# Row sums in four column strips, and a reordered tail, in a decode block of attention plus bilinear GLU

## The chip, the cores and the metric

One core of one Trainium2 chip. The metric is device microseconds of the whole program, median of several runs, lower is better. All data is fp32.

## The reference, cut to what matters

```
x: [2, 1, 512]; 32 heads of 128; the last W = 2048 of 8192 cached positions are used
xn = layernorm(x)
q  = xn @ wq                                     # 512 x 4096
p  = softmax(q . k / sqrt(128)) per head         # k, v: 2 x 32 x 2048 x 128
A  = (p . v, heads side by side) @ wo            # 4096 x 512
Bf = ((xn @ w_gate) * (xn @ w_up)) @ w_down      # 512 x 1376, 1376 x 512
return x + A + Bf                                # 2 x 512
```

With two rows of x, nearly all of the work is reading k, v and the weights once: 159 MB.

## The kernel before

**The stream.** All weights and both caches lie in DRAM as one array, already in the order in which they are used. `loads()` is a table written by hand: each step n names a buffer and the fields that one DMA brings. A field is a k or v block of one head (4,096 columns of 128 partitions), a 512-column piece of `wq`, the 128 rows of `wo` that belong to one head (512 columns), or a 128-row piece of `w_down` (`wd`, 512 columns, 256 KB). Three buffers `step0` to `step2` of 13,824 columns take turns, and a smaller one, `extra`, is used twice. All these DMAs go through SP's one queue in the order of the table; `issue(upto)` puts them into the program, and each waits until the readers of the columns that it overwrites are done.

**Scores.** For each head VectorE multiplies the k block by the query (`products`, "step<-step,q") and sums over 128 elements (`sums`, "s<-step"). After four heads (a group g) `weights(g)` finds a maximum, with one matmul into PSUM tile `tr` ("tr<-both,ones"), and ScalarE takes the exponentials (p).

**Values.** `weigh(h)` is eight TensorE matmuls of 512 columns; they write four strips of 32 partitions of an `o_ps` bank in turn. When a group is complete, `fold` copies the bank to SBUF (ScalarE, "o_sb<-o_ps"), `gather` picks the rows with four matmuls ("gu<-cst,o_sb"), and `scaled` multiplies by the reciprocal sums ("oT<-gu,rec").

**Row sums.** The products with `wo` and `wd` are added up in PSUM in two ways. `add_rows` is one matmul of 512 columns, whose two output rows stand in partitions 0 and 1 of tile `acc`. `add_groups` is four matmuls of 128 columns, which write four 32-partition strips of `acc_g`, the first 128 columns of bank `q0`. Near the end VectorE adds `acc` and x into `acc_sb`, and `add_groups` with a 2x2 identity adds that to `acc_g`, which is what leaves the chip.

**Tail.** Step 21 brings V25, V26, V27 (and wo 26, 27, wd 3), step 22 V28 and V29 (and wo 28 to 31), step 23 V30 into `extra`, and step 24 V31 and then six wd pieces in three DMAs, into the columns of buffer 0 where K30 and K31 were. The code from line 557 on is the order of TensorE's work there. Each engine runs its instructions in the order of the code.

In the trace every instruction has line 197 (the recorder's), so groups are told apart by their tiles.

Of the kernel before, what the change touches and what calls it, by code (L numbers as in the profile page):

```python
# [4 lines left out]
AF = mybir.ActivationFunctionType  # L5
ALU = mybir.AluOpType
# [4 lines left out]
P = 128  # L11
B, D, H, DH, SK, F = 2, 512, 32, 128, 8192, 1376
W = min(4096, max(256, SK // 4))
HB = P // B
# [12 lines left out]
N = B * HG  # L27
M = 4 * N
CK, CO = J * DH, D
CX = B * NC + 4 * N + 4 * HG + 2 * NFB + 2  # L30
BUFS = 3
WIDTH = 13824
WIDTH_X = 4096
# [2 lines left out]
def loads():  # L36


    def units(kind, *ids):
        w = {"k": CK, "v": CK, "wo": CO, "wd": CO, "wq": HG * DH}[kind]  # L40
        return [(kind, i, w) for i in ids]

    def wq(g, *cs):
        return units("wq", *[(g, c) for c in cs])

    big = {
        1: units("k", 0, 1, 2),
        3: units("k", 3, 4) + units("v", 0),
        4: units("k", 5, 6) + units("v", 1),
        5: units("k", 7, 8) + units("v", 2),  # L50
    }
    k, v = 9, 3
    for n in range(6, 20):
        i = 1 + n % 2
        big[n] = units("k", *range(k, k + i)) + units("v", *range(v, v + 3 - i))
        k, v = k + i, v + 3 - i
    big[20] = units("k", 30, 31) + units("v", 24)
    big[21] = units("v", 25, 26, 27)
    big[22] = units("v", 28, 29)
    small = {  # L60
        1: wq(1, 0, 1, 2),
        3: wq(1, 3) + wq(2, 0, 1),
        4: wq(2, 2, 3) + units("wd", 0),
        5: wq(3, 0, 1, 2),
        6: units("wo", 0, 1, 2),
        7: wq(3, 3) + units("wo", 3) + wq(4, 0),
        8: units("wo", 4, 5, 6),
        9: units("wo", 7) + wq(4, 1, 2),
        10: wq(4, 3) + wq(5, 0, 1),
        11: units("wo", 8, 9, 10),  # L70
        12: units("wo", 11) + wq(5, 2, 3),
        13: wq(6, 0, 1, 2),
        14: units("wo", 12, 13, 14),
        15: units("wo", 15) + wq(6, 3) + wq(7, 0),
        16: units("wo", 16, 17, 18),
        17: units("wo", 19) + wq(7, 1, 2),
        18: wq(7, 3) + units("wd", 1, 2),
        19: units("wo", 20, 21, 22),
        20: units("wo", 23, 24, 25),
        21: units("wo", 26, 27) + units("wd", 3),  # L80
        22: units("wo", 28, 29, 30, 31),
    }
    out = [
        (0, "x", [("c", 0, CX)] + wq(0, 0, 1, 2, 3)),
        (1, 0, big[1] + small[1]),
        (2, 1, [(w, 0, NC * F) for w in ("wg", "wu")]),
        (3, 2, big[3] + small[3]),
    ]
    for n in range(4, 23):
        out += [(n, (1, 0, 2)[(n - 4) % 3], big[n] + small[n])]  # L90
    out += [
        (23, "x", units("v", 30)),
        (24, 0, units("v", 31)),
        (24, 0, units("wd", 4, 5)),
        (24, 0, units("wd", 6, 7)),
        (24, 0, units("wd", 8, 9)),
    ]
    return out
# [136 lines left out]
def build(nc, stream, x_nat, wd_rest, out):  # L235
# [2 lines left out]

    buf = [pr.sb(f"step{i}", [P, WIDTH]) for i in range(BUFS)]
    buf_x = pr.sb("extra", [P, WIDTH_X])  # L240
    xr = pr.sb("xr", [B, D])
    wr = pr.sb("wr", [FR, D])
    ones = pr.sb("ones", [P, P])
    mean_w = pr.sb("mean_w", [P, P])
    eps_t = pr.sb("eps", [P, 1])
    zero = pr.sb("zero", [P, 1])
    st = pr.sb("st", [P, 4, B])
    xc = pr.sb("xc", [P, B, NC])
    sq = pr.sb("sq", [P, B, NC])
    xn = pr.sb("xn", [P, NC, B])  # L250
    xnb = pr.sb("xnb", [P, NC, P])
    cst = pr.sb("cst", [P, CX])
# [9 lines left out]
    o_sb = [pr.sb(f"o_sb{i}", [P, FB]) for i in range(2)]  # L262
    h_sb = pr.sb("h_sb", [P, FB])
    hT = pr.sb("hT", [P, 4, NFB, B])
    acc_sb = pr.sb("acc_sb", [B, D])
    o_out = pr.sb("o_out", [P, P])

    o_ps = [pr.ps(f"o_ps{i}", [P, FB]) for i in range(2)]
    q_ps = [pr.ps(f"q{i}", [P, FB]) for i in range(2)]
    acc_t = pr.ps("acc", [P, FB])  # L270
    tr = pr.ps("tr", [P, FB])
    gu_ps = [pr.ps(f"gu{i}", [P, FB]) for i in range(2)]
    hT_ps, pk_ps = gu_ps
# [19 lines left out]

    issue(3)
    pr.load("ACT", wr, wd_rest)
    pr.load("ACT", xr, x_nat)

    dve.memset(mean_w, 1.0 / D)
    dve.memset(eps_t, EPS)
    dve.memset(zero, 0.0)  # L300
    dve.memset(ones, 1.0)
    dve.memset(mt, 0.0)
    dve.memset(both, 0.0)
    for t in gu_ps:
        dve.memset(t, 0.0)
    pool.memset(p_all, 0.0)

    c0 = got["c", 0]
    dve.tensor_copy(cst, c0)
    cut = [0]  # L310
    for w in (B * NC, 4 * N, 4 * HG, 2 * NFB, 2):
        cut.append(cut[-1] + w)
    xT = cst[:, cut[0] : cut[1]].rearrange("p (b c) -> p b c", b=B)
    pick = cst[:, cut[1] : cut[2]].rearrange("p (r n) -> p r n", r=4)
# [4 lines left out]
    id2 = cst[:B, cut[4] : cut[5]]  # L319

    dve.tensor_reduce(st[:, 0, :], xT, axis=AX.X, op=ALU.add)
    pe.matmul(tr[:, 0:B], mean_w, st[:, 0, :], start=True, stop=True)
    dve.tensor_tensor(
        xc, xT, tr[:, 0:B].unsqueeze(2).to_broadcast([P, B, NC]), op=ALU.subtract
    )
    dve.tensor_tensor(sq, xc, xc, op=ALU.mult)
    dve.tensor_reduce(st[:, 1, :], sq, axis=AX.X, op=ALU.add)
    pe.matmul(tr[:, 0:B], mean_w, st[:, 1, :], start=True, stop=True)
    act.activation(st[:, 2, :], tr[:, 0:B], AF.Sqrt, bias=eps_t)
    dve.reciprocal(st[:, 3, :], st[:, 2, :])  # L330
    dve.tensor_tensor(
        xn, xc.rearrange("p b c -> p c b"),
        st[:, 3, :].unsqueeze(1).to_broadcast([P, NC, B]), op=ALU.mult,
    )
    dve.tensor_copy(
# [72 lines left out]
    def fold(g):  # L408
        act.copy(o_sb[g % 2], o_ps[g % 2])
# [10 lines left out]
            oT[g % 2][:, lo:hi], pk_ps[:, lo:hi], rec[g % 2][:, lo:hi], op=ALU.mult  # L420
        )

    acc, acc_g = acc_t[:B, :], q_ps[(NG - 2) % 2][:, 0:P]
    n_acc, n_grp = 0, 0

    def add_rows(lhsT, rhs, last=False):
        nonlocal n_acc
        pe.matmul(acc, lhsT, rhs, start=(n_acc == 0), stop=last)
        n_acc += 1
# [33 lines left out]
    def turn():  # L463
        dve.tensor_copy(
            hT.rearrange("p i n b -> p (i n b)"), hT_ps[:, 0 : 4 * B * NFB]
        )
        add_rows(hT[:FR, NFC % 4, NFC // 4, :], wr)

    def down(c, add, **kw):
        add(hT[:, c % 4, c // 4, :], got["wd", c], **kw)  # L470

    def wo(h, add, **kw):
        g, hh = divmod(h, HG)
        add(oT[g % 2][:, B * hh : B * hh + B], got["wo", h], **kw)

    def score(h):
        products(h)
# [32 lines left out]
    for n in range(3, 21):  # L510
        ks, vs = has(n, "k"), has(n, "v")
        for h in late_wo:
            wo(h, add_rows)
        late_wo = []
        full = None
        for h in vs:
            if n > 3:
                weigh(h)
            if h % HG == HG - 1:
                full = h // HG  # L520
                fold(full)
        open_q += [(n, i) for i in has(n, "wq")]
        projections(ks[0] - 1)
        for c in has(n, "wd"):
            down(c, add_rows)
        if full is not None:
            gather(full)
        for x, h in enumerate(ks):
            products(h)
            if open_g is not None:  # L530
                denominators(open_g)
                open_g = None
            if n == 3 and x == 0:
                turn()
            projections(h)
            sums(h)
            if n == 20 and x == 1:
                weigh(25)
                weigh(26)
            if h % HG == HG - 1:  # L540
                weights(h // HG)
                open_g = h // HG
                if open_g:
                    reciprocals(open_g - 1)
            if x == 0 and full is not None:
                scaled(full)
                for i in range(full * HG, full * HG + HG):
                    if i in has(n, "wo") or i in has(n - 1, "wo"):
                        wo(i, add_rows)
# [13 lines left out]
    reciprocals(g)  # L563
    gather(g - 1)
    scaled(g - 1)
    down(3, add_rows)
    for h in GROUPS[g - 1]:
        wo(h, add_rows, last=(h == a - 1))
    issue(99)
    dve.tensor_tensor(acc_sb, acc, xr, op=ALU.add)  # L570
    weigh(a)
    add_groups(id2, acc_sb)
    weigh(b)
    weigh(c, last=True)
    fold(g)
    gather(g, 0, N - B)
    scaled(g, 0, N - B)
    for h in (a, b, c):
        wo(h, add_groups)
    weigh(d, bank=0, first=True)  # L580
    fold(0)
    for i in range(4, 6):
        down(i, add_groups)
    gather(0, N - B, N)
    scaled(g, N - B, N)
    for i in range(6, 8):
        down(i, add_groups)
    wo(d, add_groups)
    for i in range(8, NFC):
        down(i, add_groups, last=(i == NFC - 1))  # L590
    dve.tensor_copy(o_out, acc_g)
    pr.load("SP", out, o_out)
    pr.emit()
# [2 lines left out]
def laid_out(x):  # L596
# [16 lines left out]
        for b in range(B):  # L613
            xs[32 * n + b, o + n * B + b] = 1.0
    o += 2 * NFB
    for b in range(B):
        xs[b, o + b] = 1.0
# [58 lines left out]
```

## Time and profile before

| | |
|---|---|
| runs | 378.11, 378.38, 380.7 us; median 378.38 us |
| profiled execution | 378.41 us, span of the core 377.1 us |
| TensorE busy | 202.7 us (54%) |
| VectorE busy | 302.1 us (80%) |
| ScalarE busy | 15.1 us (4%) |
| SP's DMA queue | 159.35 MB, 98.2% of the span of 16 engines |
| mean granted TensorE clock | 0.718 |

Times in views of the trace are microseconds from the start of the span. 1.3 us of the program's time lie around the span (378.41 against 377.1). An fp32 matmul has two records in the trace, so "x16" of `o_ps` is one `weigh`. A row of the timeline has start, length, engine, operation, output and inputs with their shapes, and in brackets the idle time ahead of it and what ended it.

### The profile page before, as it was taken

The page shows a single profiled execution, that of the slowest core. Times are in us where ns is not written, and L with a number is a line of the kernel's source. Part 1 is how long each engine was busy: PE and PEld are TensorE (multiplying, and loading weights), DVE is VectorE, ACT ScalarE, POOL GpSimd, SP SyncE. Part 2 cuts the span into 40 slices and gives each one's busy share as a digit, 9 for nine tenths or more (in the row PEclk, how much of TensorE's full clock was granted, in tenths as well). Part 3 has the DMA queues.
Part 4 walks back from the last instruction along what each step waited for, and adds up shares of the span by engine and source line. Part 5 has one row for each costly group of instructions (what it writes and reads, how often), then busy time and mean ns, then how long its engine had stood idle before and what let it go on. Part 6 is the DMA issues. An engine that isn't in the chain of part 4 may idle for free.

```text
span 377.1 us, 2019 instructions
## 1 busy us (share of the span) xinstructions
PE 202.7 (54%) x880; PEld 59.3 (16%) x880; DVE 302.1 (80%) x165; ACT 15.1 (4%) x29; POOL 2.0 (1%) x5
## 2 busy tenths in 40 slices
PE   1651847623753557816457093381666374541996
PEld 1210122100220112101112020110111011010324
DVE  2059979999999987999599399969969995999400
ACT  1000100000000000000100000000000001000101
POOL 2000000000000000000000000000000000000000
PEclk9966756586685856858569756876568586675899
DMA  8999899998999999999999999999999999999994
GB/s 324 469 393 487 375 469 452 389 469 387 458 458 393 458 422 424 463 393 452 452 401 458 399 452 458 405 442 428 422 463 405 440 458 401 452 411 451 404 410 195
DMA packets 4300, 159.68 MB, mean 423 GB/s; under 512 B 482, under 2 KB 610, under 8 KB 1092
## 3 DMA queue, kind: packets, MB, share of 16 engines
q1 hardware_dynamic: 4176, 159.35, 98.2%
q10 hardware_dynamic: 116, 0.20, 0.2%
q8 instruction: 7, 0.11, 0.1%
q14 instruction: 1, 0.01, 0.0%
HBM read 159.49 MB, written 0.07 MB: 423 GB/s over the span
## 4 chain that ended last, share of the span: by engine, by line
DVE 44%; DMA 42%; PE 11%; issue 1%; another core or an unknown queue 1%; ACT 0%; SPq 0%; DVEq 0%
DMA step<-in_stream_dram 42%; DVE step L197 22%; DVE s L197 20%; PE acc L197 4%; PE o_ps L197 4%; PE q L197 2%; PE gu L197 1%; ACT o_sb L197 0%; PE tr L197 0%; DVE both L197 0%; DVE nm L197 0%; DVE h_sb L197 0%; DVE mt L197 0%; DVE mtt L197 0%
## 5 line engine op out<-in xcount | busy, mean ns | idle before, releaser
L197 DVE TENSOR_TENSOR step<-step,q 128x4096 f32<-128x4096 f32 x32 | 141.1, 4408 | 38.5 <-DMA step<-in_stream_dram 38.5
L197 DVE TENSOR_REDUCE s<-step 128x32 f32<-128x4096 f32 x32 | 141.4, 4418 | 0.8
L197 PE MATMUL o_ps<-step,p 128*32 128x512 f32 x496 | 89.4, 819 | 71.7 <-DMA step<-in_stream_dram 70.1
L197 PE MATMUL acc<-step,oT 128*2 128x512 f32 x56 | 39.7, 868 | 33.5 <-DVE oT L197 29.2
L197 PE MATMUL q<-step,xnb 128*128 128x512 f32 x56 | 40.6, 863 | 26.5 <-DVE step L197 18.9
L197 PEld LDWEIGHTS o_ps<-step,p 128*32 128x32 f32 x496 | 19.1, 139 | 123.3 <-DMA step<-in_stream_dram 76.9
L197 PEld LDWEIGHTS q<-step,xnb 128*128 128x128 f32 x56 | 13.4, 266 | 52.5 <-DVE step L197 24.1
L197 ACT ACTIVATE p<-s,zero 64x128 f32<-64x128 f32 x16 | 6.4, 399 | 266.9 <-DVE s L197 266.8
L197 PEld LDWEIGHTS acc<-step,oT 128*2 128x2 f32 x56 | 5.2, 105 | 62.0 <-DVE oT L197 30.1
L197 PE MATMUL gu<-step,xn 128*2 128x512 f32 (+1 forms) x48 | 9.7, 728 | 7.8 <-DMA step<-in_stream_dram 7.8
L197 PE MATMUL gu<-cst,o_sb 128*128 128x8 f32 (+2 forms) x72 | 9.5, 258 | 3.9 <-ACT o_sb L197 3.8
L197 PE MATMUL tr<-both,ones 128*128 128x24 f32 (+1 forms) x18 | 4.3, 317 | 12.7 <-DVE both L197 12.7
L197 DVE TENSOR_TENSOR oT<-gu,rec 128x8 f32<-128x8 f32 (+2 forms) x9 | 1.4, 159 | 12.1 <-PE gu L197 12.1
L197 PEld LDWEIGHTS gu<-cst,o_sb 128*128 128x128 f32 x72 | 8.7, 191 | 12.1 <-ACT o_sb L197 10.4
L197 DVE TENSOR_REDUCE nm<-tr 64x4 f32<-64x8 f32 x16 | 2.6, 163 | 6.6 <-PE tr L197 6.5
L197 ACT COPY o_sb<-o_ps 128x512 f32<-128x512 f32 x9 | 5.3, 585 | 49.8 <-PE o_ps L197 49.8
L197 PEld LDWEIGHTS tr<-both,ones 128*128 128x128 f32 x18 | 3.3, 229 | 23.3 <-DVE both L197 22.5
L197 PE MATMUL q<-extra,xnb 128*128 128x512 f32 x8 | 5.7, 878 | 1.2 <-DVE xnb L197 1.2
L197 PE MATMUL tr<-st,mean_w 128*128 128x2 f32 x4 | 1.2, 364 | 7.8 <-DVE st L197 7.8
L197 PEld LDWEIGHTS gu<-step,xn 128*2 128x2 f32 x48 | 2.2, 99 | 15.7 <-DMA step<-in_stream_dram 9.1
L197 PE MATMUL gu<-cst,h_sb 128*128 128x6 f32 x8 | 1.9, 362 | 4.4 <-DVE h_sb L197 4.4
L197 DVE TENSOR_TENSOR acc_sb<-acc,xr 2x512 f32<-2x512 f32 x1 | 0.7, 678 | 4.2 <-PE acc L197 4.2
(48 smaller groups left out, 43.8 us busy)
## 6 DMA issues: line engine op xcount, KB each, us to landing
step<-in_stream_dram SPq DMA_DIRECT2D x20, 6912.0 KB, 31.0
step<-in_stream_dram SPq DMA_DIRECT2D x1, 5504.0 KB, 34.4
step<-in_stream_dram SPq DMA_DIRECT2D x1, 5120.0 KB, 26.8
extra<-in_stream_dram SPq DMA_DIRECT2D x1, 2048.0 KB, 31.4
step<-in_stream_dram SPq DMA_DIRECT2D x1, 2048.0 KB, 28.0
step<-in_stream_dram SPq DMA_DIRECT2D x3, 512.0 KB, 21.4
extra<-in_stream_dram SPq DMA_DIRECT2D x1, 1056.0 KB, 6.0
wr<-in_wd_rest_dram ACTq DMA_DIRECT2D x1, 192.0 KB, 5.5
```

The source lines that it names most:

```text
L197: ins = getattr(e, method)(*args, **kw)
```

## The change

1. **Four strips.** `acc` is now a whole bank, zeroed at the start. `add_rows` takes a strip number j and writes partitions 32j and 32j+1; every wo row takes the strip of its head within the group (h % 4), except that heads 24, 25 and 26 take strip 0 and head 27 strip 1. `xr` (x, zero elsewhere), `acc_sb` and the identity (`id4`, two constant columns) stretch over 128 partitions.
2. **The final addition.** In the tail all wo rows but head 31's, and wd 1 to 7, go through `add_rows`. VectorE's addition of `acc` and x and `add_groups(id4, acc_sb)` come last, behind wd 8 and 9.
3. **wo rows of heads 26 and 27** go behind `fold(g)`, ahead of the gather that waits for that copy.
4. **Order of the stream.** wd 1 and 2 leave step 18, wd 3 leaves step 21; they come behind V31. The three last DMAs bring four, three and two pieces where each brought two.
5. **Four spare matmuls** (`keep_busy`) ahead of V25: 512 columns each, into a bank that nobody reads, with the scores of K30 as weights, so they wait for these.
6. **Layer norm** in one pass: sums of x minus a pivot and of its square go through one matmul instead of two in a row; two more constant columns hold the pivot.
7. **Memsets** of `zero`, `mt`, `both` and the new one of `xr` are on GpSimd, ahead of that of p; the load of x waits for the memset of `xr`.

```
         17: units("wo", 19) + wq(7, 1, 2),
-        18: wq(7, 3) + units("wd", 1, 2),
+        18: wq(7, 3),
...
-        21: units("wo", 26, 27) + units("wd", 3),
+        21: units("wo", 26, 27),
...
         (24, 0, units("v", 31)),
-        (24, 0, units("wd", 4, 5)),
-        (24, 0, units("wd", 6, 7)),
+        (24, 0, units("wd", 1, 2, 3, 4)),
+        (24, 0, units("wd", 5, 6, 7)),
         (24, 0, units("wd", 8, 9)),
...
+    spare = q_ps[(NG - 2) % 2]
+    n_acc, n_grp = [0] * 4, 0
+    def add_rows(lhsT, rhs, j, last=False):
+        pe.matmul(
+            acc[32 * j : 32 * j + B, :], lhsT, rhs, start=(n_acc[j] == 0), stop=last
+        )
+        n_acc[j] += 1
...
+    def keep_busy(behind, times):
+        for _ in range(times):
+            pe.matmul(
+                spare[:HB // 2, :], behind, xnb.rearrange("p c k -> p (c k)"),
+                start=True, stop=True,
+            )
...
             if n == 20 and x == 1:
+                keep_busy(s_t[1][:, 2, :], 4)
                 weigh(25)
                 weigh(26)
...
     scaled(g - 1)
-    down(3, add_rows)
-    for h in GROUPS[g - 1]:
-        wo(h, add_rows, last=(h == a - 1))
+    wo(a - 4, add_rows, 0)
+    wo(a - 3, add_rows, 0)
     issue(99)
-    dve.tensor_tensor(acc_sb, acc, xr, op=ALU.add)
     weigh(a)
-    add_groups(id2, acc_sb)
     weigh(b)
     weigh(c, last=True)
     fold(g)
+    wo(a - 2, add_rows, 0)
+    wo(a - 1, add_rows, 1)
     gather(g, 0, N - B)
     scaled(g, 0, N - B)
     for h in (a, b, c):
-        wo(h, add_groups)
+        wo(h, add_rows, h % HG)
     weigh(d, bank=0, first=True)
     fold(0)
-    for i in range(4, 6):
-        down(i, add_groups)
+    for i in range(1, 5):
+        down(i, add_rows, i % 4, last=(i == 4 - 1))
     gather(0, N - B, N)
     scaled(g, N - B, N)
-    for i in range(6, 8):
-        down(i, add_groups)
+    for i in range(5, 8):
+        down(i, add_rows, (i - 5), last=True)
+    dve.tensor_tensor(acc_sb, acc, xr, op=ALU.add)
     wo(d, add_groups)
     for i in range(8, NFC):
-        down(i, add_groups, last=(i == NFC - 1))
+        down(i, add_groups)
+    add_groups(id4, acc_sb, last=True)
     dve.tensor_copy(o_out, acc_g)
```

The order of the instructions shows this at three places. First TensorE from V24 (the first row below) to the wo rows of group 6; "-" is before, "+" is the change, and "hT" are the inputs of `wd`:

```order
-L197 MATMUL o_ps<-step,p 32x512 x24
+L197 MATMUL o_ps<-step,p 32x512 x8
+L197 MATMUL q<-xnb,s 32x512 x4
+L197 MATMUL o_ps<-step,p 32x512 x16
 L197 MATMUL tr<-both,ones 128x24
 L197 MATMUL o_ps<-step,p 32x512 x8
 L197 MATMUL tr<-both,ones 128x8
 L197 MATMUL gu<-cst,o_sb 128x8 x4
-L197 MATMUL acc<-step,hT 2x512
-L197 MATMUL acc<-step,oT 2x512 x4
+L197 MATMUL acc<-step,oT 2x512 x2
```

The four spare matmuls (q<-xnb,s) stand between V24 and V25, and three of the five serial `acc` matmuls have left the place ahead of V28.

Then the end of TensorE's program before, from V30 (`extra`) on:

```order
L197 MATMUL o_ps<-extra,p 32x512 x8
L197 MATMUL gu<-cst,o_sb 128x6 x4
L197 MATMUL q<-step,oT 2x128 x12
L197 MATMUL o_ps<-step,p 32x512 x8
L197 MATMUL q<-step,hT 2x128 x8
L197 MATMUL gu<-cst,o_sb 128x2 x4
L197 MATMUL q<-step,hT 2x128 x8
L197 MATMUL q<-step,oT 2x128 x4
L197 MATMUL q<-step,hT 2x128 x8
```

and in the change:

```order
L197 MATMUL o_ps<-extra,p 32x512 x8
L197 MATMUL acc<-step,oT 2x512 x2
L197 MATMUL gu<-cst,o_sb 128x6 x4
L197 MATMUL acc<-step,oT 2x512 x3
L197 MATMUL o_ps<-step,p 32x512 x8
L197 MATMUL acc<-step,hT 2x512 x4
L197 MATMUL gu<-cst,o_sb 128x2 x4
L197 MATMUL acc<-step,hT 2x512 x3
L197 MATMUL q<-step,oT 2x128 x4
L197 MATMUL q<-step,hT 2x128 x8
L197 MATMUL q<-acc_sb,cst 2x128 x4
```

Seven wd pieces stand as rows of `acc` around the last gather where four stood as groups, and the addition of `acc_sb` is the last thing that TensorE does.

Third, SP's last loads in the change, from step 18 (12,800 columns) to the store of the output:

```order
L197 DMA step<-in_stream_dram 128x12800
L197 DMA step<-in_stream_dram 128x13824 x2
L197 DMA step<-in_stream_dram 128x13312
L197 DMA step<-in_stream_dram 128x10240
L197 DMA extra<-in_stream_dram 128x4096
L197 DMA step<-in_stream_dram 128x4096
L197 DMA step<-in_stream_dram 128x2048
L197 DMA step<-in_stream_dram 128x1536
L197 DMA step<-in_stream_dram 128x1024
L197 DMA out_dram<-o_out 128x128
```

Steps 18 and 21 are 1,024 and 512 columns shorter, and the 1,536 columns stand again in the loads behind V31 (2,048, 1,536 and 1,024 where there were three of 1,024).

More of the change, by code (lines that the diff above doesn't have):

```diff
@@ L29 @@
 CK, CO = J * DH, D
-CX = B * NC + 4 * N + 4 * HG + 2 * NFB + 2
+CX = B * NC + 4 * N + 4 * HG + 2 * NFB + 2 + B
 BUFS = 3
@@ L240, in build @@
     buf_x = pr.sb("extra", [P, WIDTH_X])
-    xr = pr.sb("xr", [B, D])
+    xr = pr.sb("xr", [P, D])
     wr = pr.sb("wr", [FR, D])
@@ L247, in build @@
     st = pr.sb("st", [P, 4, B])
-    xc = pr.sb("xc", [P, B, NC])
-    sq = pr.sb("sq", [P, B, NC])
+    xc = pr.sb("xc", [P, 2, B, NC])
     xn = pr.sb("xn", [P, NC, B])
@@ L264, in build @@
     hT = pr.sb("hT", [P, 4, NFB, B])
-    acc_sb = pr.sb("acc_sb", [B, D])
+    acc_sb = pr.sb("acc_sb", [P, D])
     o_out = pr.sb("o_out", [P, P])
@@ L269, in build @@
     q_ps = [pr.ps(f"q{i}", [P, FB]) for i in range(2)]
-    acc_t = pr.ps("acc", [P, FB])
+    acc = pr.ps("acc", [P, FB])
     tr = pr.ps("tr", [P, FB])
@@ L295, in build @@
     pr.load("ACT", wr, wd_rest)
-    pr.load("ACT", xr, x_nat)
     dve.memset(mean_w, 1.0 / D)
     dve.memset(eps_t, EPS)
-    dve.memset(zero, 0.0)
     dve.memset(ones, 1.0)
-    dve.memset(mt, 0.0)
-    dve.memset(both, 0.0)
-    for t in gu_ps:
+    for t in gu_ps + [acc]:
         dve.memset(t, 0.0)
-    pool.memset(p_all, 0.0)
+    for t in (xr, zero, mt, both, p_all):
+        pool.memset(t, 0.0)
+    pr.load("ACT", xr[:B, :], x_nat)
     c0 = got["c", 0]
@@ L310, in build @@
     cut = [0]
-    for w in (B * NC, 4 * N, 4 * HG, 2 * NFB, 2):
+    for w in (B * NC, 4 * N, 4 * HG, 2 * NFB, 2, B):
         cut.append(cut[-1] + w)
@@ L318, in build, with per_row @@
     sel = cst[:, cut[3] : cut[4]]
[L319 to L324, printed above, removed]
-    )
[L326 to L329, printed above, removed]
+    id4 = cst[:, cut[4] : cut[5]]
+    pivot = cst[:, cut[5] : cut[6]]
+    def per_row(ap):
+        return ap.unsqueeze(2).to_broadcast([P, B, NC])
+    xd, sq = xc[:, 0], xc[:, 1]
+    dve.tensor_tensor(xd, xT, per_row(pivot), op=ALU.subtract)
+    dve.tensor_tensor(sq, xd, xd, op=ALU.mult)
+    dve.tensor_reduce(st[:, 0:2, :], xc, axis=AX.X, op=ALU.add)
+    pe.matmul(
+        tr[:, 0 : 2 * B], mean_w, st[:, 0:2, :].rearrange("p s b -> p (s b)"),
+        start=True, stop=True,
+    )
+    dve.tensor_tensor(xd, xd, per_row(tr[:, 0:B]), op=ALU.subtract)
+    dve.tensor_copy(st[:, 0:2, :].rearrange("p s b -> p (s b)"), tr[:, 0 : 2 * B])
+    dve.tensor_tensor(st[:, 2, :], st[:, 0, :], st[:, 0, :], op=ALU.mult)
+    dve.tensor_tensor(st[:, 1, :], st[:, 1, :], st[:, 2, :], op=ALU.subtract)
+    act.activation(st[:, 2, :], st[:, 1, :], AF.Sqrt, bias=eps_t)
     dve.reciprocal(st[:, 3, :], st[:, 2, :])
     dve.tensor_tensor(
-        xn, xc.rearrange("p b c -> p c b"),
+        xn, xd.rearrange("p b c -> p c b"),
         st[:, 3, :].unsqueeze(1).to_broadcast([P, NC, B]), op=ALU.mult,
@@ L421, in scaled @@
         )
[L423 to L429, printed above, removed]
+    spare = q_ps[(NG - 2) % 2]
+    acc_g = spare[:, 0:P]
+    n_acc, n_grp = [0] * 4, 0
[4 more added lines that the diff above has]
+        n_acc[j] += 1
     def add_groups(lhsT, rhs, last=False):
@@ L466, in turn, with down, wo @@
         )
[L467 to L472, printed above, removed]
+        add_rows(hT[:FR, NFC % 4, NFC // 4, :], wr, 0)
+    def down(c, add, *args, **kw):
+        add(hT[:, c % 4, c // 4, :], got["wd", c], *args, **kw)
+    def wo(h, add, *args, **kw):
         g, hh = divmod(h, HG)
-        add(oT[g % 2][:, B * hh : B * hh + B], got["wo", h], **kw)
+        add(oT[g % 2][:, B * hh : B * hh + B], got["wo", h], *args, **kw)
+    def keep_busy(behind, times):
+        for _ in range(times):
+            pe.matmul(
+                spare[:HB // 2, :], behind, xnb.rearrange("p c k -> p (c k)"),
+                start=True, stop=True,
+            )
     def score(h):
@@ L512, in build @@
         for h in late_wo:
-            wo(h, add_rows)
+            wo(h, add_rows, h % HG)
         late_wo = []
@@ L524, in build @@
         for c in has(n, "wd"):
-            down(c, add_rows)
+            down(c, add_rows, 1)
         if full is not None:
@@ L548, in build @@
                     if i in has(n, "wo") or i in has(n - 1, "wo"):
-                        wo(i, add_rows)
+                        wo(i, add_rows, i % HG)
                     else:
@@ L578, in build @@
     for h in (a, b, c):
-        wo(h, add_groups)
+        wo(h, add_rows, h % HG)
     weigh(d, bank=0, first=True)
     fold(0)
-    for i in range(4, 6):
-        down(i, add_groups)
+    for i in range(1, 5):
+        down(i, add_rows, i % 4, last=(i == 4 - 1))
     gather(0, N - B, N)
     scaled(g, N - B, N)
-    for i in range(6, 8):
-        down(i, add_groups)
+    for i in range(5, 8):
+        down(i, add_rows, (i - 5), last=True)
+    dve.tensor_tensor(acc_sb, acc, xr, op=ALU.add)
     wo(d, add_groups)
     for i in range(8, NFC):
-        down(i, add_groups, last=(i == NFC - 1))
+        down(i, add_groups)
+    add_groups(id4, acc_sb, last=True)
     dve.tensor_copy(o_out, acc_g)
@@ L615, in laid_out @@
     o += 2 * NFB
-    for b in range(B):
-        xs[b, o + b] = 1.0
+    for j in range(4):
+        for b in range(B):
+            xs[32 * j + b, o + b] = 1.0
+    xs[:, o + 2 :] = a[:, 0]
     cache = {
```

## The prediction

> **What bounds the kernel now.** I read the queue section of the page first, then the page's summary of the chain that ended last.
>
> ```profile
> q1 hardware_dynamic: 4176, 159.35, 98.2%
> DVE 44%; DMA 42%; PE 11%; issue 1%; another core or an unknown queue 1%; ACT 0%; SPq 0%; DVEq 0%
> ```
>
> SP's queue is at work for 98.2% of the span. The second row seems to say that VectorE is the bound, but a chain follows one release after another; where the queue never empties, the share of DVE in it costs nothing. So I read the chain in order of time (start, length, what).
>
> ```profile
> 308.73 38.89 DMA step<-in_stream_dram
> ...
> 347.66 5.86 PE o_ps L197 x32
> ...
> 357.47 3.96 PE acc L197 x9
> ...
> 363.90 3.62 PE o_ps L197 x32
> ...
> 370.32 1.76 PE o_ps L197 x16
> ...
> 373.80 1.25 PE q L197 x40
> ...
> 375.07 0.29 DVE o_out L197
> ```
>
> Step 21 (V25 to V27) lands at 308.73 + 38.89 = 347.62. Two loads earlier, step 19 released VectorE (the timeline's row):
>
> ```profile
> 314.95 4.42 DVE L197 TENSOR_TENSOR step<-step,q 128x4096 f32<-128x4096 f32 x1 [3.78 <-DMA step<-in_stream_dram]
> ```
>
> So two loads of 13,824 columns came in 347.62 - 314.95 = 32.7 us: 16.34 us each, or 0.605 us for 512 columns. From 347.62 on the chain is all TensorE. But it is hardly ahead of the transfers there, as the issues and their times to landing show (timeline rows, then rows of the DMA view of single stretches: KB, us to landing).
>
> ```profile
> 332.91 0.33 SPq L197 DMA_DIRECT2D step<-in_stream_dram  x1
> 333.28 0.43 SPq L197 DMA_DIRECT2D extra<-in_stream_dram  x1
> 341.69 10.06 SPq L197 DMA_DIRECT2D step<-in_stream_dram  x4
> ```
>
> ```profile
> step<-in_stream_dram SPq DMA_DIRECT2D x1, 5120.0 KB, 26.8
> extra<-in_stream_dram SPq DMA_DIRECT2D x1, 2048.0 KB, 31.4
> step<-in_stream_dram SPq DMA_DIRECT2D x1, 2048.0 KB, 28.0
> step<-in_stream_dram SPq DMA_DIRECT2D x1, 512.0 KB, 22.1
> ```
>
> ```profile
> L197 SPq DMA_DIRECT2D step<-in_stream_dram x26: 327/328/647, 1.2 to 351.3; - x26
> ```
>
> V28 lands at 332.91 + 26.8 = 359.7, V30 at 333.28 + 31.4 = 364.7, V31 at 341.69 + 28.0 = 369.7. The last row gives the start of the last load, 351.3, so wd 8 and 9 land at 351.3 + 22.1 = 373.4. The chain turns to V31 at 370.32, 0.6 us behind its landing, and ends its matmuls at 375.05, 1.6 us behind the last landing. So in the tail two lines run side by side, TensorE's and the queue's, and TensorE's is the later one by about half a microsecond. Whatever shortens TensorE by more than that meets the queue.
>
> **The change: the queue.** The stream carries the same fields, and 1 KB more of constants (8 bytes for each of 128 rows). Its end stays at 373.4. What moves is the order: three pieces ahead of V25 go behind V31. Everything from step 18 to V31 lands earlier by 0.605 us a piece: 1.21 us for steps 18 to 20, 1.82 us from step 21 on. V25 then lands at 345.8, V28 at 357.9, V30 at 362.9, V31 at 367.9. Behind V31 the pieces fill what is left up to 373.4, at 5.5 / 9 = 0.61 us each: wd 1 to 4 at 370.4, wd 5 to 7 at 372.2, wd 8 and 9 at 373.4. SP issues V31 when K30's scores are done and the wd loads when K31's are; both are over 20 us ahead of their landings, so no wait of SP reaches the queue.
>
> **The change: the spare matmuls and V25 to V27.** VectorE and TensorE meet at the maximum of the last group.
>
> ```profile
> 346.02 4.42 DVE L197 TENSOR_REDUCE s<-step 128x32 f32<-128x4096 f32 x1
> 351.26 0.23 DVE L197 TENSOR_SCALAR both<-cst,mc 128x16 f32<-128x16 f32 x1
> 353.45 0.40 PE L197 MATMUL tr<-both,ones 128*128 128x24 f32 x2
> 324.15 4.78 PE L197 MATMUL acc<-step,oT 128*2 128x512 f32 x6 [3.98 <-DVE oT L197]
> ```
>
> The wait for step 19 (the row at 314.95) now ends 1.2 us earlier; behind that it works without a pause, so K31's sums end at 349.2 instead of 350.44 and `both` is ready at 350.3 instead of 351.49. In the run before, TensorE came to that matmul only at 353.45, because V25 and V26 took 5.86 us (first chain row), against 3.62 us for two heads later on.
>
> ```profile
> 348.80:352.20 3.40, 3.40 (x20) 0.79 (x16) 2.56 (x5) 0.00 (x0) 0.00 (x0) 0.50 0.98 422
> 352.20:355.60 3.40, 3.40 (x30) 0.84 (x22) 0.99 (x5) 0.80 (x2) 0.00 (x0) 1.00 0.89 386
> 205.42:208.84 3.42, 1.54 (x4) 0.38 (x2) 3.38 (x2) 0.00 (x0) 0.00 (x0) 1.00 0.93 404
> 208.84:212.25 3.41, 0.00 (x0) 0.00 (x0) 2.12 (x1) 0.00 (x0) 0.00 (x0) 1.00 0.94 405
> 212.25:215.66 3.41, 0.00 (x0) 0.00 (x0) 0.00 (x0) 0.00 (x0) 0.00 (x0) 0.50 1.13 486
> ```
>
> These stretches show why (the granted clock is the third number from the end; the first behind the length is TensorE's busy time): 0.50 until a stretch of 3.4 us was busy throughout, then 1.00; and 1.00 kept through a stretch that was 45% busy, lost after one that was idle. Four spare matmuls are eight records; the six `acc` records in 4.78 us were about 0.86 us each at the low clock, so the spare ones take at most 6.9 us from 340.4 (K30's scores), to 347.3, and include at least one whole stretch: V25 and V26 then run at the high clock, 3.6 us. They end between 349.4 and 350.9, and the matmul for the maximum starts between 350.3 and 350.9 instead of 353.45. From there to the end of the gather took 357.47 - 353.45 = 4.0 us, so 354.9 at the latest; two wo rows in one strip are four records of 0.44 us (nine took 3.96), with 0.3 us for `scaled` 2.1 us. TensorE stands at V28 by 357.0, and V28 lands at 357.9. **It waits from here on**, so the gain of the spare matmuls and of the three rows taken out (2.6 us) buys nothing beyond these 0.9 us of slack.
>
> **The change: V28 to V31.** Durations come from these rows.
>
> ```profile
> 363.83 1.92 PE L197 MATMUL o_ps<-step,p 128*32 128x512 f32 x16
> 36.11 9.73 PE L197 MATMUL gu<-step,xn 128*2 128x512 f32 x48 [7.80 <-DMA step<-in_stream_dram]
> 372.11 0.58 ACT L197 COPY o_sb<-o_ps 128x512 f32<-128x512 f32 x1 [3.99 <-PE o_ps L197]
> 372.75 1.05 PE L197 MATMUL gu<-cst,o_sb 128*128 128x2 f32 x8 [0.27 <-ACT o_sb L197]
> 371.86 0.62 PE L197 MATMUL q<-step,hT 128*2 128x128 f32 x16
> 361.89 0.68 DVE L197 TENSOR_TENSOR acc_sb<-acc,xr 2x512 f32<-2x512 f32 x1 [4.22 <-PE acc L197]
> ```
>
> One head of `weigh` is 1.92 us for eight matmuls in four strips. The second row has the form of the new row sums: two output rows, 512 columns, three strips. One after another its 48 records would take 48 x 0.44 = 21 us; they took 9.73 us, half of it at the low clock. So strips overlap with two rows too, and I take 0.9 us for up to four wo or wd rows in different strips (two records of 0.43 us); the other end, no overlap, is a rival. V28 and V29 from 357.9 end at 361.5; V30 from 362.9 at 364.8. wo 26 and 27 take 0.9 us while the copy takes 0.6, so the gather starts at 365.7, and with `scaled` and three wo rows TensorE is done at 367.9, when V31 lands.
>
> From V31 at 367.9: `weigh` to 369.8, copy to 370.45. TensorE waits for wd 1 to 4 until 370.4, adds them by 371.3; gather to 372.35; wd 5 to 7 (landed 372.2) to 373.25; VectorE's addition, now over 128 partitions but still 512 elements each, 0.7 us, to 374.0. Meanwhile wo 31 and wd 8 and 9 (0.3 and 0.62 us) end at 374.15, and the addition through `id4` (four matmuls of that form, half of 0.62, and the way to VectorE: 0.35) at 374.5. **The copy to `o_out` starts at 374.5 instead of 375.07: 0.57 us earlier.** A second way gives the same: last landing 373.4, two pieces 0.62, `id4` 0.35, some 0.1 between.
>
> The Trainium skill, page "TensorE: Matmul & The Clock Gate", section "Measured speedup vs the span model", speaks against part of this: three column tiles gave 2.38 times there, not three. By it wd 5 to 7 would take 1.1 us, about 0.2 us more, and the program 378.0 us; of `acc` in three strips no run here shows the duration.
>
> **The change: edits at nothing.** Layer norm, memsets and the later load of x lie ahead of the first k block:
>
> ```profile
> 23.14 4.42 DVE L197 TENSOR_TENSOR step<-step,q 128x4096 f32<-128x4096 f32 x1 [12.99 <-DMA step<-in_stream_dram]
> ```
>
> VectorE had been idle for 12.99 us when K0 came, and of these the first projection of q (eight records of 0.86 us at most) takes 6.9: about 6 us are left before K0 would feel it. One matmul less stands against three small VectorE operations more, and x is not read before the last addition. wo rows in mid-stream use less of TensorE, which is not late there.
>
> **The sum.** 378.41 - 0.57 = 377.84 us against the profiled execution, which is 0.03 us from the median of 378.38: **377.8 us**, 0.15% below before, inside what a measurement of this kernel can tell from no change, about 1%. Bounds within this case: a clock that falls for one stretch in the new waits +0.5 (the wo rows and one gather at half speed, the rest of it in slack), and 0.4 either way for landings that I know to 0.1 us each. Its own range is 377.2 to 378.7.
>
> **The rivals.**
>
> *The clock goes cold in the new waits (slower).* TensorE now waits about 0.9 us for V28 and 1.4 us for V30, and where a stretch of 3.4 us falls below the 45% that held the clock, V31 starts at 0.50. Then `weigh` is 3.5 us, wd 1 to 4 1.7, the gather up to 2.1; with a whole busy stretch behind it the clock is back 3.4 to 6.8 us after V31. That puts the copy 1.7 to 2.8 us behind my 374.5: 379.5 to 380.6 us. Against it: I find no stretch of 3.4 us from 357.9 on with less than 1.9 us of work (56%). The Trainium skill, same page, section "What's actually happening", asks for an idle window of 3.4 us; the rows above agree, and no wait here is that long. It decides from a stretch under half busy before 368. Chance 0.06.
>
> *The stream slows.* Every load now starts 1 KB later in DRAM, and the first has rows of 8,456 bytes. From a slowdown of 0.16% (0.6 us of 372) the gain is gone; 1% gives 381.5. For it: nothing but that no load here started off the old grid. Against it: 5,120 KB took 359.7 - 347.62 = 12.1 us, at the rate of the 6,912 KB loads, though its rows are shorter; the rate doesn't hang on the form. Chance 0.09.
>
> *Strips with two rows don't overlap, so the change does not do what it says.* wo 26 and 27 then take 1.7 us, three rows 2.6, four 3.4: 0.9 + 1.7 + 2.6 + 1.7 less 1 us of cover puts the end 5 to 6 us behind mine, 383.5 us. The `gu` row speaks against it. Chance 0.04.
>
> *TensorE alone decided (faster).* If transfers are early enough everywhere, its own savings count: 353.45 - 350.4 = 3.0, three rows 2.6, the first `acc_sb` addition 0.3, less 0.9 for the longer end: 5 us, 373.4 us. Against it stands the last landing, 373.4, which allows no copy before 374.4. It needs a faster stream. Chance 0.07.
>
> **How the numbers follow.** Forecast 0.74, rivals 0.06, 0.09, 0.04, 0.07. Faster by over 1% (below 374.6) is the last rival, 0.07. Slower by over 1% (above 382.2) is the third and most of the second, which can be any size: 0.04 + 0.07 = 0.11. Within 1% is the rest, 0.82. The range reaches from 376.6 (half a microsecond of faster stream or a cheaper end) to 380.6, the upper end of the cold tail; slower streams and the two outer rivals are left out.
>
> **What would show each step.** Right: V25 lands near 345.8, V31 near 367.9, the last load still at 373.4; V25 and V26 in under 4 us at clock 1.00; TensorE idle ahead of V28 and V30 "<-DMA"; four wd rows in about 0.9 us; `o_out` at 374.5. The chain should show DMA, not TensorE, up to V31. Wrong: landings 16.4 us or more apart in mid-stream, a clock of 0.50 anywhere behind 358, or `acc` records that follow each other at 0.43 us in different strips.

## The result

The change runs in 377.89 us, median of 20 runs (377.68 to 378.08), against 378.47 us before (377.91 to 381.31, 20 runs): ratio 0.9967, 95% interval 0.9951 to 0.9983. The ratio is of means, and 6 of the 20 runs before lie between 380.7 and 381.3 us, where none of the change's does; the medians differ by 0.15%. Profiled execution: 377.87 us, span 376.5 us (before 378.41 and 377.1). The page of the change, queue section and summary of the chain:

```profile
q1 hardware_dynamic: 4176, 159.35, 98.3%
DVE 54%; DMA 40%; PE 4%; issue 1%; another core or an unknown queue 1%; SPq 0%; DVEq 0%
```

TensorE's share of the chain has fallen from 11% to 4%. The chain in order of time, its end:

```profile
349.41 20.93 DMA step<-in_stream_dram
370.34 0.04 issue
370.38 1.04 PE acc L197 x8
371.42 0.98 PE gu L197 x8
...
373.43 0.70 DVE acc_sb L197
...
374.17 0.45 PE q L197 x8
...
374.64 0.29 DVE o_out L197
```

Where before it was TensorE's from 347.62 on, it now is a transfer's until 370.34: the landing of wd 1 to 4. The copy to `o_out` starts at 374.64 instead of 375.07. The issues of V28, V30 and V31 on SP and the times to landing (rows of single stretches; the last is that of wd 8 and 9):

```profile
331.84 0.33 SPq L197 DMA_DIRECT2D step<-in_stream_dram  x1
332.22 0.42 SPq L197 DMA_DIRECT2D extra<-in_stream_dram  x1
340.63 10.06 SPq L197 DMA_DIRECT2D step<-in_stream_dram  x4
```

```profile
step<-in_stream_dram SPq DMA_DIRECT2D x1, 5120.0 KB, 26.2
extra<-in_stream_dram SPq DMA_DIRECT2D x1, 2048.0 KB, 30.7
step<-in_stream_dram SPq DMA_DIRECT2D x1, 2048.0 KB, 27.2
step<-in_stream_dram SPq DMA_DIRECT2D x1, 512.0 KB, 23.2
```

So V28 lands at 358.0 (before 359.7), V30 at 362.9 (364.7), V31 at 367.8 (369.7), and the last load, issued at 350.3, at 373.5 (373.4). TensorE in the timeline:

```profile
340.65 5.86 PE L197 MATMUL q<-xnb,s 128*32 128x512 f32 x8 [5.34 <-DVE s L197]
346.00 3.95 PE L197 MATMUL o_ps<-step,p 128*32 128x512 f32 x32
350.49 0.40 PE L197 MATMUL tr<-both,ones 128*128 128x24 f32 x2 [0.54 <-DVE both L197]
354.77 1.88 PE L197 MATMUL acc<-step,oT 128*2 128x512 f32 x4 [0.26 <-DVE oT L197]
358.11 3.64 PE L197 MATMUL o_ps<-step,p 128*32 128x512 f32 x32 [1.47 <-DMA step<-in_stream_dram]
363.01 1.92 PE L197 MATMUL o_ps<-extra,p 128*32 128x512 f32 x16 [1.26 <-DMA extra<-in_stream_dram]
364.75 1.03 PE L197 MATMUL acc<-step,oT 128*2 128x512 f32 x4
367.02 1.03 PE L197 MATMUL acc<-step,oT 128*2 128x512 f32 x6 [0.26 <-DVE oT L197]
367.89 1.92 PE L197 MATMUL o_ps<-step,p 128*32 128x512 f32 x16
```

The rows are the spare matmuls, V25 and V26, the maximum, wo 24 and 25, V28 and V29, V30, wo 26 and 27 in the pause (the time of `fold`'s copy, in which TensorE would wait for the gather's input), wo 28 to 30, V31. TensorE is idle for 1.47 and 1.26 us ahead of V28 and V30, "<-DMA" both times. The three wo rows (six records, 367.02) take 0.87 us until V31 starts; one after another they would take 2.6.

### The profile page after: what moved, and what is told of

The parts are those of the page before. It is cut to its first block, busy times and chain, and to the rows that moved or that the text cites. A ratio compares the mean times of both kernels' runs of the same rounds, so it can differ in the third digit from the quotient of the medians.

```text
span 376.5 us, 1954 instructions
## 1 busy us (share of the span) xinstructions
PE 194.0 (52%) x844; PEld 57.2 (15%) x844; DVE 302.9 (80%) x166; ACT 15.1 (4%) x29; POOL 2.6 (1%) x9
## 3 DMA queue, kind: packets, MB, share of 16 engines
q1 hardware_dynamic: 4176, 159.35, 98.3%
## 4 chain that ended last, share of the span: by engine, by line
DVE 54%; DMA 40%; PE 4%; issue 1%; another core or an unknown queue 1%; SPq 0%; DVEq 0%
DMA step<-in_stream_dram 40%; DVE step L197 27%; DVE s L197 25%; PE acc L197 2%; PE q L197 1%; DVE both L197 1%; PE tr L197 1%; DVE nm L197 0%; PE gu L197 0%; DVE mt L197 0%; DVE acc_sb L197 0%; DVE h_sb L197 0%; DVE mtt L197 0%; DVE rec L197 0%
## 5 line engine op out<-in xcount | busy, mean ns | idle before, releaser
L197 PE MATMUL o_ps<-step,p 128*32 128x512 f32 x496 | 95.4, 866 | 57.0 <-DMA step<-in_stream_dram 55.4
L197 PE MATMUL acc<-step,oT 128*2 128x512 f32 x62 | 23.7, 893 | 43.9 <-DVE oT L197 27.8
L197 PEld LDWEIGHTS o_ps<-step,p 128*32 128x32 f32 x496 | 21.1, 147 | 113.1 <-DMA step<-in_stream_dram 62.2
L197 PEld LDWEIGHTS acc<-step,oT 128*2 128x2 f32 x62 | 1.6, 82 | 54.0 <-DVE oT L197 28.5
L197 PE MATMUL q<-xnb,s 128*32 128x512 f32 x8 | 5.9, 903 | 5.3 <-DVE s L197 5.3
```

The source lines that it names most:

```text
L197: ins = getattr(e, method)(*args, **kw)
```

## Experiments

**Is it the order of the stream?** Theory: the landings of V31 and of the last load set the end. Rival: the gain is TensorE's shorter program (strips, pause, spare matmuls).

*The spare matmuls taken out.*

```
             if n == 20 and x == 1:
-                keep_busy(s_t[1][:, 2, :], 4)
```

> The change without its four spare matmuls; all else as in the change. Theory (the queue sets the end: V31 lands at 367.9 and the last load at 373.4 whatever TensorE does before): V25 and V26 run at the low clock at first, the matmul for the maximum starts at about 352 instead of 350.5, V28 starts within 0.5 us of its landing at 358, and the copy to o_out stays at 374.6; 377.9 us. Rival (the warm clock is what brings the gain): everything behind V25 is later by the 1.5 to 2 us, the copy at 375 or later, 378.4 us or more.

Measured: 377.85 us (377.77 to 378.00, 12 runs). V25, the maximum and V28 in its timeline:

```profile
345.94 5.79 PE L197 MATMUL o_ps<-step,p 128*32 128x512 f32 x32 [11.51 <-DMA step<-in_stream_dram]
351.66 0.40 PE L197 MATMUL tr<-both,ones 128*128 128x24 f32 x2
358.06 3.64 PE L197 MATMUL o_ps<-step,p 128*32 128x512 f32 x32 [0.24 <-DMA step<-in_stream_dram]
```

V25 and V26 take 5.79 us instead of 3.95, the maximum is 1.2 us later, and V28 starts when it lands, as in the change: the wait of 1.47 us has become one of 0.24. The spare matmuls buy nothing here.

*The old order of the stream in the changed program.*

```
-        18: wq(7, 3),
+        18: wq(7, 3) + units("wd", 1, 2),
-        21: units("wo", 26, 27),
+        21: units("wo", 26, 27) + units("wd", 3),
-        (24, 0, units("wd", 1, 2, 3, 4)),
-        (24, 0, units("wd", 5, 6, 7)),
+        (24, 0, units("wd", 4, 5)),
+        (24, 0, units("wd", 6, 7)),
...
+    down(3, add_rows, 3, last=True)          # behind scaled(g - 1)
...      # in words: wd 4, 5 as rows in the pause of fold(0), wd 6, 7 as rows behind the last gather
```

> The change with the stream order of before: wd 1 and 2 in step 18, wd 3 in step 21, and wd 4 to 9 in three loads of two pieces behind V31; strips, spare matmuls and the late addition as in the change. Theory (queue order): V31 lands at 369.7 again, and the long end behind it (weigh, copy, gather, rows, addition through 128 partitions, final groups) ends 0.9 to 1.0 us later than in the change: copy to o_out at 375.6, 378.8 us, slower than before. Rival (TensorE's shorter program brings the gain): the time of the change, 377.9 us, or at most 0.3 us more.

Measured: 378.97 us (378.90 to 379.04, 12 runs), 1.1 us above the change and above most runs of before (median 378.58 of 35 runs on the same chip, 12 of them over 380 us). From its chain (V31's matmuls, rows of wd 4 and 5, `o_out`), and V28 and V29 in its timeline:

```profile
369.90 1.72 PE o_ps L197 x16
371.62 0.85 PE acc L197 x4
...
375.67 0.29 DVE o_out L197
```

```profile
359.73 5.34 PE L197 MATMUL o_ps<-step,p 128*32 128x512 f32 x32 [2.04 <-DMA step<-in_stream_dram]
```

`o_out` starts at 375.67, where 375.6 was expected. Strips, pause and spare matmuls alone lose 0.4 us in the median: V31 lands when it did, its matmuls stand 0.4 us earlier in the chain than before (369.90 against 370.32), but from there to `o_out` it is 5.8 us instead of 4.8 (rows, addition over 128 partitions, `id4`). The last row shows a cost that does not reach the end: behind a wait of 2.04 us the granted clock is 0.50 from 360.23 to 363.65, V28 and V29 take 5.34 us instead of the change's 3.64. V30 lands only at 364.7 and starts at 364.9, so that nearly all of it is hidden.

*The new order of the stream in the old program.*

```
-        18: wq(7, 3) + units("wd", 1, 2),
+        18: wq(7, 3),
-        21: units("wo", 26, 27) + units("wd", 3),
+        21: units("wo", 26, 27),
-        (24, 0, units("wd", 4, 5)),
-        (24, 0, units("wd", 6, 7)),
+        (24, 0, units("wd", 1, 2, 3, 4)),
+        (24, 0, units("wd", 5, 6, 7)),
...
-    down(3, add_rows)
...      # in words: wd 1 to 4 and 5 to 7 as groups where 4, 5 and 6, 7 were
```

> The kernel before with the new stream order alone (wd 1 to 9 behind V31 in loads of four, three and two pieces, added in groups where 4 to 9 were); no strips, no spare matmuls, serial rows, addition of acc and x where it was. Theory (queue order): V25 to V31 land 1.2 to 1.8 us earlier; TensorE, with one wd row less, reaches V28 at 359.2 and V31 at 368.4, 0.5 us behind its landing, and ends 4.9 + 1.2 us of matmuls later: copy at 374.5 to 374.7, 377.8 us (to 378.3 where the clock of V25 and V26 stays low longer). Rival (strips, the pause and the spare matmuls bring the gain): 378.3 us, as before.

Measured: 378.22 us (377.36 to 378.94, 12 runs). The middle is 0.4 us above the 377.8 expected, but five runs are at 378.17 or less, two are below every run of the change, and none is near 381. V31 in its timeline (an execution of 377.90 us):

```profile
368.14 3.18 PE L197 MATMUL o_ps<-step,p 128*32 128x512 f32 x16
```

V31 took 3.18 us instead of 1.92: its granted clock is 0.50 from 367.29 to 370.70, as in the runs of the next part. The copy to `o_out` starts at 374.66, inside the 374.5 to 374.7 expected, but the expectation had V31 at the high clock, so that hit is in part luck. Had V31 taken 1.9 us, the last landing and wd 8 and 9 (373.4 and 0.62) would put the copy at about 374.1 and the time at about 377.4 us; this is an estimate from these rows, and the shortest run (377.36) was not profiled.

The four medians on this chip are 378.58 us for before, 378.97 for the new program with the old order, 378.22 for the old program with the new order, and 377.85 for both together (without the spare matmuls). In the new program the order is worth 1.1 us; alone it brings about half of the change's gain in the median, and only 0.1 us against before's runs under 380 us (median 378.32). So the theory holds for the new program, but neither part alone gives the change's time. One thing each part does alone: none of its 12 runs is near 381. On record, with the long runs counted, the ratio to before is 0.9975 (0.9952 to 0.9997) for the program with the old order, 0.9966 (0.9943 to 0.9990) for the order alone, and 0.9961 (0.9938 to 0.9984) for both.

**Why before has runs near 381.** Theory: the granted clock falls while TensorE is at V31. Rival: transfers.

*Before, unchanged.*

> The kernel before, unchanged, for the spread of its runs: some lie near 380.9 us, 2.5 us above the others, and none of the change's does. Theory (its tail is TensorE's, and the clock's free-running windows fall differently from run to run): the long runs show a lower mean granted clock. Rival (transfers): the long runs have the same mean clock, and the change would show such runs too in as many runs.

Measured: six runs from 378.03 to 378.76 us and six from 380.61 to 381.47. The profiled one took 380.93 us. Stretches of it that follow the steps of the clock, then V25 and V26 and V31:

```profile
363.87:367.28 3.41, 3.41 (x35) 0.91 (x36) 0.00 (x0) 0.00 (x0) 0.00 (x0) 1.00 0.96 404
367.28:370.70 3.42, 2.46 (x36) 1.45 (x32) 0.16 (x1) 0.58 (x1) 0.00 (x0) 1.00 0.97 393
370.70:374.11 3.41, 3.41 (x36) 1.25 (x28) 0.00 (x0) 0.00 (x0) 0.00 (x0) 0.50 0.36 144
```

```profile
347.93 6.45 PE L197 MATMUL o_ps<-step,p 128*32 128x512 f32 x32 [13.60 <-DMA step<-in_stream_dram]
366.42 1.90 PE L197 MATMUL o_ps<-extra,p 128*32 128x512 f32 x16
369.02 1.06 PE L197 MATMUL gu<-cst,o_sb 128*128 128x6 f32 x8 [0.71 <-ACT o_sb L197]
370.34 1.16 PE L197 MATMUL q<-step,oT 128*2 128x128 f32 x24 [0.26 <-DVE oT L197]
371.26 3.32 PE L197 MATMUL o_ps<-step,p 128*32 128x512 f32 x16
```

The clock is 0.50 from 370.70 to 374.11, and V31 takes 3.32 us instead of 1.90; V25 and V26 took 0.6 us more than in the first profile. With 0.3 us more in the wo groups (1.16 against 0.84) and 0.3 us in the landing of V25 that is the 2.5 us. All later loads landed within 0.3 us of the first profile's times, V31 at 369.9 and so 1.4 us before TensorE came to it; it is not the transfers. This is the only long run of before that has a profile. My sign was wrong, though: the mean clock (0.721) is no lower, since a fall of 3.4 us hardly shows in 380.

The stretch that lost the clock was 2.46 of 3.42 us busy. But 1.06 of that is the gather, which streams six columns a matmul. Without it, V30 until 368.32 and the wo groups from 370.34 leave 1.40 us, 41%. The share of a stretch in which matmuls of 128 or 512 columns run is called streaming below.

*The pause filled before.* One spare matmul ahead of the gather.

```
     fold(g)
+    pe.matmul(q_ps[1][:M, :], p_all[:, 0, 0, 0, :], xnb.rearrange("p c k -> p (c k)"),
+              start=True, stop=True)
     gather(g, 0, N - B)
```

> The kernel before with one spare matmul of 512 columns (32 output rows, into a bank that nobody reads any more) in the pause of the copy ahead of the gather of heads 28 to 30. Theory (clock): 0.2 us longer than the pause, so 0.1 to 0.2 us on the usual runs, 378.2 to 379.0 us, but no run near 381: the stretch ahead of V31 gains 0.25 of streaming. Rival (the long runs come from the transfers or elsewhere): about a third of the runs still lie at 380.5 to 381.5 us.

Measured: 378.17 us (377.75 to 379.10, 12 runs), none near 381, where 5 of 35 runs of before on the same chip were (and 29 of all 102). The spare matmul and V31 in its profile, an execution of 378.70 us:

```profile
367.62 1.02 PE L197 MATMUL q<-xnb,p 128*32 128x512 f32 x2
370.54 1.90 PE L197 MATMUL o_ps<-step,p 128*32 128x512 f32 x16
```

By the counts this points to the clock; with 5 of 35 it would be no proof alone.

*The pause emptied in the change.* wo 26 and 27 back ahead of V28.

```
     wo(a - 3, add_rows, 0)
+    wo(a - 2, add_rows, 0)
+    wo(a - 1, add_rows, 1)
...
     fold(g)
-    wo(a - 2, add_rows, 0)
-    wo(a - 1, add_rows, 1)
     gather(g, 0, N - B)
```

> The change with the wo rows of heads 26 and 27 back in their old place behind those of 24 and 25, ahead of V28, so that the pause of the copy ahead of the gather is empty. Theory (the clock is kept by matmuls that stream 512 columns; a gather that streams 8 hardly counts): in the runs where a free-running stretch of 3.4 us starts within about 1 us of the end of V30's matmuls it holds less than 42% of streaming, the clock falls to 0.50 as V31 lands, and weigh takes 3.3 us instead of 1.9; runs at 377.9 us and, about 3 in 10 of them, at 379 to 379.8 us. Rival (the wait for V31 and the gather leave the clock alone; the long runs of before had another cause): all runs within 0.3 us of 377.9.

Measured: seven runs from 377.77 to 378.04 us and five from 378.46 to 378.91. The profiled one was short, so two more were profiled.

> A second profile of the version with the empty pause, for its longer runs (378.46 to 378.91 us in five of twelve). Theory (clock): if this one is long, the view by stretches shows 0.50 while V31 is weighed, which then takes over 2.5 us instead of 1.92, with all landings as before; if it is short (below 378.1 us), the clock is 1.00 there. Rival (transfers): a long one has the clock at 1.00 and V31 or a later load landing 0.5 us or more later.

> A third profile of the version with the empty pause; the same as for the second.

Both were long, 378.62 and 378.68 us. Of the first, the stretches, V31, and V31's issue and time to landing:

```profile
363.86:367.27 3.41, 2.45 (x23) 1.16 (x18) 0.17 (x1) 0.59 (x1) 0.00 (x0) 1.00 0.98 416
367.27:370.69 3.42, 3.42 (x19) 1.30 (x17) 0.00 (x0) 0.00 (x0) 0.00 (x0) 0.50 1.00 412
```

```profile
367.85 3.47 PE L197 MATMUL o_ps<-step,p 128*32 128x512 f32 x16
340.54 10.06 SPq L197 DMA_DIRECT2D step<-in_stream_dram  x4
step<-in_stream_dram SPq DMA_DIRECT2D x1, 2048.0 KB, 27.3
```

V31 lands at 340.54 + 27.3 = 367.8 as in the change, and takes 3.47 us at a clock of 0.50; in the other one 3.46 us. In the first stretch V30 streams until 364.85 and the wo rows from 366.88: 1.38 us, 40%; the gather makes up the rest of the 2.45. The price was 0.8 us, not the 1.1 to 1.9 expected: 1.5 us more of V31, of which the wait for wd 1 to 4 (0.57 us in the change) and the shorter waits behind it hid half. So wo 26 and 27 in the pause are worth 0.8 us in 5 of 12 runs, by keeping the clock, not by the time they save elsewhere.

*The spare matmuls in the old program.*

```
             if n == 20 and x == 1:
+                for _ in range(4):
+                    pe.matmul(q_ps[0][: HB // 2, :], s_t[1][:, 2, :],
+                              xnb.rearrange("p c k -> p (c k)"), start=True, stop=True)
                 weigh(25)
```

> The kernel before with the four spare matmuls ahead of V25 as the only edit. Theory (the queue): V25 and V26 take 3.9 us instead of 5.8, but V28 lands at 359.7, V30 at 364.6 and V31 at 369.7, so TensorE gains at most 0.4 us by the end: 378.0 us in the usual runs; the pause ahead of V31 is as it was, so long runs near 381 stay. Rival (TensorE decides the tail): 2 us less, 376.4 us.

Measured: eight runs from 377.75 to 378.13 us, four from 379.27 to 379.70. V25 and V26, then V30, in an execution of 377.75 us:

```profile
347.66 3.72 PE L197 MATMUL o_ps<-step,p 128*32 128x512 f32 x32
364.67 1.92 PE L197 MATMUL o_ps<-extra,p 128*32 128x512 f32 x16 [0.79 <-DMA extra<-in_stream_dram]
```

V25 and V26 gain 2.1 us, V30 then waits for its landing, and `o_out` starts at 374.52, 0.55 us earlier than in the first profile: the queue again, and not the 2 us of the rival. In the medians it is 0.2 us (377.99 against 378.19 on this chip). The long runs lie at 379.5, where 381 was expected; that fits V25 and V26 being no longer part of them.

> A second profile of the kernel before with spare matmuls ahead of V25, for its longer runs (379.27 to 379.70 us in four of twelve). Theory (clock): if this one is long, the clock is 0.50 while V31 is weighed and weigh takes over 3 us; if it is short (below 378.2 us), the clock is 1.00 there. Rival (transfers): a long one has later landings and the clock at 1.00.

It took 377.92 us, a short one, so the long ones of this version were not seen in a profile; that they are the clock is not shown, only argued from the two kernels beside it.

**A shorter end.** If the last landing sets the end, little must follow it.

```
-        4: wq(2, 2, 3) + units("wd", 0),
+        4: wq(2, 2, 3),
-        22: units("wo", 28, 29, 30, 31),
+        22: units("wo", 28, 29, 30),
...      # in words, the loads behind V31:
-        # three: wd 1-4, wd 5-7, wd 8-9
+        # five: wd 0-1 and wo 31, wd 2-5, wd 6-7, wd 8, wd 9
...      # in words: wo 27 to strip 3; acc_sb = acc + xr ahead of weigh(d);
...      # behind fold(0): wd 0, 1 and acc_sb as groups; gather; wd 2-5, wo 31, wd 6-9 as groups
```

> A version of the change with a shorter end: wd 0 and wo 31 go behind V31 too (eleven pieces, in loads of three, four, two, one and one), acc and x are added while V31 is weighed and go to the groups in the pause of the last copy, and wd 0 to 9 are groups, so that behind the last landing one piece is left. Theory (the end is the last landing, 373.4, and what must follow it): V31 lands at 366.6, the last gather ends at 370.4, the pieces are added as they land, copy to o_out at 373.9 to 374.1 instead of 374.64: 377.2 us. Rival (the line behind V31 sets the end, not the last landing): V31 lands 1.2 us earlier, so 1.2 us less or more, 376.7 us or below; a third, that small loads are slow: 377.9 us or more.

Measured: 377.31 us (377.13 to 377.53, 12 runs), 0.9972 of before, interval 0.9960 to 0.9984 (its 35 runs of before on that chip had fewer long ones, median 378.19). It is 0.1 us above the 377.2 expected and faster than both kernels: 0.6 us below the change's 377.89, which was measured on another chip, and on the same chip below the shortest run, 377.77, of the version with the empty pause. The end of its chain:

```profile
350.58 22.96 DMA step<-in_stream_dram
373.59 0.44 PE q L199 x8
374.05 0.29 DVE o_out L199
```

The chain is one transfer up to 373.54, one wd piece, the copy. Rival one (the line behind V31, 1.2 us) is out: V31 is 1.2 us earlier and the end 0.6. So is the third, slow small loads (377.9 us or more). Behind a queue that is at work for 98.5% of the span, only one piece, the copy and the store are left.

## Why the prediction was right, point by point

- **The bound** held: the last load lands at 373.5 in the change, and the two orders of the stream move the new program as V31's landing and the work behind it say. In the old program the granted clock ahead of V31 decides as well.
- **Landings**: V28 358.0, V30 362.9, V31 367.8 against 357.9, 362.9, 367.9. 0.605 us a piece was right.
- **Spare matmuls**: warm V25 and V26 in 3.95 us (3.6 forecast, part of the spare records still ran beside them), the maximum at 350.49 (350.3 to 350.9), and worth nothing, as the run without them shows.
- **Waits** of 0.9 and 1.4 us ahead of V28 and V30 were 1.47 and 1.26: TensorE was at V28 0.4 us earlier than the latest time I had used. So the rival "TensorE alone decided" is out: time saved ahead of V28 turns into waiting, and the spare matmuls in the old program gave 0.2 to 0.55 us, not 2.
- **Strips** overlap: 0.87 us for three rows; wd 1 to 4 take 0.97 until the gather. The 2.38 times that the Trainium skill gives (page "TensorE: Matmul & The Clock Gate", section "Measured speedup vs the span model"; by it, 1.1 us for three, an estimate) is not what these strips show: 2.6 / 0.87 is three times. The rival without overlap is out.
- **The end**: `o_out` at 374.64 against 374.5. The 0.14 us lies in the last term: `id4` starts at 374.17, where 374.15 was forecast, and takes 0.47 us to the copy instead of 0.35. It was released by VectorE's addition (373.43 to 374.13, 0.1 us later than forecast), and not by wd 8 and 9, whose matmuls end just before.
- **The sum**: 377.87 us for the profiled execution against 377.84, and 377.89 against 377.8. To agree within 0.03 us is luck: the copy came 0.14 us later than forecast, and around and behind it the program took 0.1 us less than before (377.87 - 374.64 = 3.23 against 378.41 - 375.07 = 3.34).
- **The rival "clock goes cold" stood in the wrong kernel.** Its point of decision, half a stretch busy, counted the gather as work. By streaming, before drops to 41% ahead of V31 in its profiled long run, and that fall is 1.4 of the 2.5 us. The reason that I gave against the rival, that no wait is as long as 3.4 us, does not hold either: in the run with the old order a stretch with a wait of 2.04 us, 40% busy, lost the clock. In the change, wo 26 and 27 (364.75) and three 512-column wo rows (367.02) stand there, and the clock is 1.00 throughout:

```profile
364.60:368.00 3.40, 3.15 (x26) 1.27 (x24) 0.16 (x1) 0.59 (x1) 0.00 (x0) 1.00 0.97 407
368.00:371.40 3.40, 2.83 (x28) 0.47 (x24) 0.00 (x0) 0.59 (x1) 0.00 (x0) 1.00 0.97 396
```

  I had not looked for what the change does to the spread of the runs, and it is half of the measured ratio: 0.15% between medians, 0.33% between means. The spread was in the runs shown (380.7 us), and I passed over it.
- **The stream slows**: no. 98.3% of the span, and the last landing within 0.1 us.

## What to carry to other kernels

Where a queue never empties, ask of each transfer what still has to be done behind it, and send first what has the longest work behind it: three pieces moved behind V31 are worth 1.1 us in a program whose TensorE is ready when V31 lands, and 0.1 to 0.4 us in one that is not. A stall that TensorE spends on a copy is not only its own length: filled with matmuls that stream many columns, it keeps the clock for what comes next. And a median of three with one run 0.6% off hides a second mode; profile a run of that one too before costing the tail.

## What the runs showed of the hardware that I had not expected

The clock is lost without an idle stretch. 3.4 us in which TensorE was 2.46 us busy (41% by streaming) lost it, 1.54 us of 3.42 (45%, all of it 512-column matmuls) held it. Counting only matmuls of 128 or 512 columns, in the 13 traces taken no whole stretch above 47% lost the clock and none below 40% held it; between the two, both happened. By busy time they are much further apart: stretches of up to 72% lost it, and some of 41% held it. The Trainium skill, page "TensorE: Matmul & The Clock Gate", section "What's actually happening", gives an idle window of about 3.4 us as the condition; the two profiles above with 40 and 41% differ from it, and the measurement decides. Where the stretches fall differs from run to run, which makes two modes of one kernel: of the 102 runs of before 72 lie between 377.7 and 379.0 us, 29 between 380.5 and 381.5.
